# Regrouping the fp32 transposes in the q, k, v stage of a gated attention and token-mixer kernel

## The chip, the cores and the metric

One core of a Trainium2 chip runs the whole kernel. The metric is the device time of one execution in microseconds (us); less is better. TensorE is called PE in the rows, VectorE DVE, ScalarE ACT, GpSimd POOL and SyncE SP; SP issues the DMAs here.

## The reference

For x of 2048 tokens by 640 channels the result is `g * a + (1 - g) * b`, with one gate g per token:

```python
g = sigmoid((x * gate_w).sum(-1, keepdims=True))
q = (x @ wq).reshape(B, S, 32, 20).transpose(0, 2, 1, 3)
k, v = x @ wk, x @ wv                      # one key and one value head, 20 wide
p = softmax(einsum("bhqd,bkd->bhqk", q, k) * 20 ** -0.5)
a = einsum("bhqk,bkd->bhqd", p, v).transpose(0, 2, 1, 3).reshape(B, S, 640) @ wo
h = layernorm(x)                           # over the channels
u = gelu(einsum("bsd,sf->bdf", h, w1) + b1)   # mixes the tokens, F = 1728
b = (einsum("bdf,fs->bds", u, w2) + b2).transpose(0, 2, 1)
```

The change touches the first two lines of this alone: the transposes of x that the projections read, and the transposes of v and of the gate's sum.

## The kernel before

The kernel runs three stages one after the other: the q, k, v stage (about the first 95 us), a lead stage, and the long attention loop into which the token mixer's matmuls are woven. All engines follow the order in which the instructions were written (a manual schedule), so each engine takes its instructions in program order, and a wait in front holds back all that stands behind it on that engine.

The q, k, v stage works on four blocks of 512 tokens (`sb`, lines 430 to 475). For each block the tokens' 640 channels, in five chunks `c` of 128, have to lie across the partitions. `transpose_x` (L312) does that on TensorE: four fp32 transposes of 128x128 fill one PSUM bank of 128x512. `split_x` (L307) then reads the bank twice, ScalarE for the high part (L309) and VectorE for the low part (L310). All matmuls of the projections take such high and low parts. `project` (L324) is a row of matmuls of 512 columns that add up in one bank.

A block goes like this. First comes `pk`, ten matmuls that give k, v and the gate's sum. `split_kv` takes them out: ScalarE copies one half (L346), VectorE adds the other (L347), and the sum lies in `kv` (blocks 0 and 1) or `kept` (blocks 2 and 3). Then five projections of q follow, m = 0 to 4. The x of the next block is turned beside them, in groups of chunks that stand ahead of a projection. After each projection `split_q` takes the one before it out (L339 on ScalarE, L340 on VectorE) and stores it. `turn_v` (L361) turns `kv` by four transposes (L364) into one bank, which is read by a copy to `v_sb` (ScalarE L368 in block 0, VectorE L366 else) and by a copy to `z_col` (VectorE L369). The layer norm of the block runs between all this on VectorE, ScalarE and POOL: its `ht` tiles (L276) share two buffers, so the third scaling waits until POOL has taken the low parts of the first (L290).

Two PSUM pools of four banks each serve the stage: `psa` (tiles `pp`, the projections and chunk 4 of x) and `pst` (tiles `pt`, the other chunks of x, and v):

```python
pts = [(pst if c < 4 else psa).tile([P, NB], F32, name="pt" if c < 4 else "pp") for c in cs]
```

In block 0 the projections m = 0 to 2 are mostly done ahead, so that the row of m = 2 has only five matmuls left, and the group of m = 3 follows that of m = 2 closely.

Of the kernel before, what the change touches and what calls it, by code (L numbers as in the profile page):

```python
# [20 lines left out]
DC = D // P  # L21
# [4 lines left out]
NQB = S // NB  # L26
# [22 lines left out]
def mix_kernel(ctx: ExitStack, tc: tile.TileContext, A_x, A_wq, A_wk, A_wv, A_wo,  # L49
# [130 lines left out]
    def new_qmax(n):  # L180
        if n < NU and n not in qmax:
            qmax[n] = load_q(n, "qmx")
# [9 lines left out]
    with tc.tile_pool(name="pa", bufs=1) as pa, \  # L192
# [9 lines left out]
        def load_x(sb):  # L202
            for st in range(4 * sb, 4 * sb + 4):
                nc.sync.dma_start(out=xts[st], in_=x[st * P:(st + 1) * P, :])
# [102 lines left out]
        def split_x(sb, c, pt):  # L307
            th, tl = x_tiles(sb, c)
            nc.scalar.activation(th, pt, AF.Copy)  # L309
            nc.vector.tensor_sub(tl, pt, f32(th))  # L310

        def transpose_x(sb, cs):  # L312
            pts = [(pst if c < 4 else psa).tile([P, NB], F32, name="pt" if c < 4 else "pp") for c in cs]
            for i in range(4):
                for c, pt in zip(cs, pts):
                    nc.tensor.transpose(pt[:, i * P:(i + 1) * P], xts[4 * sb + i][:, c * P:(c + 1) * P], ident)
            return [(sb, c, pt) for c, pt in zip(cs, pts)]

        def project(steps, pp=None, more=False):
            first = pp is None  # L320
            if first:
                pp = psa.tile([P, NB], F32, name="pp")
            for n, (w, t) in enumerate(steps):
                nc.tensor.matmul(pp, w, t, start=first and n == 0, stop=not more and n == len(steps) - 1)  # L324
            return pp

        def q_parts(m, ts):
            cols = slice(m * P, (m + 1) * P)
            return [[(wq_hi[:, c, cols], ts[c][0]) for c in range(DC)],
                    [(wq_hi[:, c, cols], ts[c][1]) for c in range(DC)],  # L330
                    [(wq_lo[:, c, cols], ts[c][0]) for c in (0, 3, 1, 4, 2)]]

        def split_q(sb, m, pp):
            if (sb, m) == (NQB - 1, DC - 1):
                qh, ql = (xin[0][:, i, :NB].bitcast(F32R) for i in range(2))
            else:
                qh = paw.tile([P, NB], F32R, name="qh")
                ql = paw.tile([P, NB], F32R, name="ql")
            nc.scalar.activation(qh, pp, AF.Copy)  # L339
            nc.vector.tensor_sub(ql, pp, f32(qh))  # L340
            for j, t in enumerate((qh, ql)):
                nc.sync.dma_start(out=q_scr[j, m * P:(m + 1) * P, sb * NB:(sb + 1) * NB], in_=f32(t))

        def split_kv(sb, pp):
            kv = kvs[max(0, sb - 1)][:64, :]
            nc.scalar.activation(kv, pp[64:, :], AF.Copy)  # L346
            nc.vector.tensor_add(kv, kv, pp[:64, :])  # L347
            k_hi = pa.tile([DH, NB], F32R, name="k_hi")
            k_lo = pa.tile([DH, NB], F32R, name="k_lo")
            nc.scalar.activation(k_hi, kv[:DH, :], AF.Copy)  # L350
            nc.gpsimd.tensor_sub(k_lo, kv[:DH, :], f32(k_hi))
            return kv, k_hi, k_lo

        def store_k(sb, k_hi, k_lo):
            cols = slice(sb * NB, (sb + 1) * NB)
            for b in range(2):
                for j, t in enumerate((k_hi, k_hi, k_lo)):
                    o = 64 * b + DH * j
                    nc.sync.dma_start(out=f32(kst[o:o + DH, cols]), in_=f32(t))

        def turn_v(sb):  # L361
            pv = pst.tile([P, 4, P], F32, name="pt")
            for i in range(4):
                nc.tensor.transpose(pv[:, i, :], kvs[max(0, sb - 1)][:, i * P:(i + 1) * P], ident)  # L364
            if sb:
                nc.vector.tensor_copy(v_sb[:, 4 * sb:4 * sb + 4, :DH], pv[:, :, 32:32 + DH])  # L366
            else:
                nc.scalar.activation(v_sb[:, :4, :DH], pv[:, :, 32:32 + DH], AF.Copy)  # L368
            nc.vector.tensor_copy(z_col[:, 4 * sb:4 * sb + 4], pv[:, :, 32 + DH])  # L369

        def turn_bias():
            pb = pst.tile([P, NB], F32, name="pt")
            nc.tensor.transpose(pb[:, :P], bb, ident)
            nc.vector.tensor_copy(bias, pb[:, :32])
# [17 lines left out]
        def first_block():  # L392
            ahead = [psa.tile([P, NB], F32, name="pp") for _ in range(QW // P)]

            def turn(c):
                nc.gpsimd.tensor_copy(wq_hi[:, c, :QW], wqs[c])
                split_x(*transpose_x(0, (c,))[0])

            nc.gpsimd.tensor_copy(wq_hi[:, 0, :QW], wqs[0])
            th, tl = x_tiles(0, 0)  # L400
            for a in range(2):
                pt = pst.tile([P, NB], F32, name="pt")
                cols = slice(a * 2 * P, (a + 1) * 2 * P)
                for i in range(2):
                    nc.tensor.transpose(pt[:, i * P:(i + 1) * P], xts[2 * a + i][:, :P], ident)
                nc.scalar.activation(th[:, cols], pt[:, :2 * P], AF.Copy)
                nc.vector.tensor_sub(tl[:, cols], pt[:, :2 * P], f32(th[:, cols]))
            for c in range(DC):
                if c == 0:
                    for i in range(2):  # L410
                        nc.tensor.matmul(warm, kst[:, :P], kst[:, :NB], start=True, stop=True)
                    first_q(c, 0, ahead)
                if c + 1 < DC:
                    turn(c + 1)
                for j in range(c == 0, 2):
                    first_q(c, j, ahead)
                wq_low(c, slice(0, QW), wqs[c])
            load_x(1)
            split_wkv()
            for c in range(DC):  # L420
                nc.scalar.activation(wq_hi[:, c, QW:], wqs2[c], AF.Copy)
            for c in (0, 3, 1, 4, 2):
                wq_low(c, slice(QW, D), wqs2[c])
            norm = layer_norm(0)
            for _ in range(3):
                next(norm)
            return ahead, norm

        due = None
        for sb in range(NQB):  # L430
            ahead, norm = first_block() if sb == 0 else ([], layer_norm(sb))
            ts = [xT[sb, c] for c in range(DC)]
            if 0 < sb < NQB - 1:
                load_x(sb + 1)
            pk = project([(wkv_s[:, c, :], t) for c in range(DC) for t in ts[c]])
            if due:
                split_q(*due)
            kv, k_hi, k_lo = split_kv(sb, pk)
            store_k(sb, k_hi, k_lo)
            if sb:  # L440
                next(norm)
            for m in range(DC):
                turned = []
                if sb + 1 < NQB and m > 1 and (sb, m) != (2, DC - 1):
                    turned = transpose_x(sb + 1, ((0, 1), (2, 3), (4,))[m - 2])
                p = q_parts(m, ts)
                if m < len(ahead):
                    pp = project(p[2], ahead[m])
                elif m < DC - 1:
                    pp = project(p[0] + p[1] + p[2])  # L450
                else:
                    pp = project([p[r][c] for c in range(DC) for r in range(3)])
                if m == (not sb):
                    turn_v(sb)
                if m:
                    split_q(*due)
                due = sb, m, pp
                for t in turned:
                    split_x(*t)
                if sb == 1 and m == 1:  # L460
                    turn_bias()
                if sb == 1 and m == 0:
                    w1_load(3)
                if sb == 2 and 0 < m < 4:
                    w1_upto(m)
                if sb == 3 and m == 1:
                    w1_upto(4)
                    new_qmax(0)
                if sb == 3 and m == 3:
                    gates()  # L470
                for _ in range(2 if sb == 0 and m == 1 else 1 + (sb and m > 1 or sb == 3)):
                    next(norm, None)
            if sb == 2:
                for t in transpose_x(3, (4,)):
                    split_x(*t)
# [721 lines left out]
    m = len(ph)  # L1197
# [304 lines left out]
```

## Time and profile before

| | |
|---|---|
| median of 3 runs | 1594.0 us (1593.82 to 1594.34) |
| the profiled execution's own time | 1594.53 us |
| its span, first to last instruction | 1592.4 us |
| TensorE (PE) busy | 1587.0 us, 100% of the span |
| VectorE (DVE) busy | 1348.2 us, 85% |
| ScalarE (ACT) busy | 1293.0 us, 81% |
| POOL busy | 866.5 us, 54% |
| mean granted TensorE clock | 1.000 |

A matmul's end is modelled and lies past the start of the next one, so in the rows below a step of TensorE is read from start to start: a matmul of 512 columns takes 0.23 us of it (eight in a row from 30.19 us to 32.06 us), though its row shows 0.4 us. A row of the timeline merges neighbours of one kind; its first number is the start of the first of them.

### The profile page before, as it was taken

Reading aid. Unit: us, or ns where it says so; the run is one execution under the profiler, and the core shown is the slowest. Engines: PE = TensorE matmul, PEld = TensorE weight load, DVE = VectorE, ACT = ScalarE, POOL = GpSimd, SP = SyncE. Lnnn points to the kernel's source line nnn. Section 1 sums busy time; section 2 is a strip of 40 time slices with the busy share of each in tenths; the row PEclk is TensorE's granted clock in tenths of the full one; section 3 lists DMA queues with packets and bytes.
Section 4 is the critical chain, followed back from the end, with each engine's and each line's share of the span. In section 5 each row is a group of like instructions: output and inputs, shape, how many; then the busy total and the mean of one; then the engine's idle time right before and its main releaser. Section 6 shows DMA issues by size and latency. Waiting matters only on the chain.

```text
span 1592.4 us, 39402 instructions
## 1 busy us (share of the span) xinstructions
PE 1587.0 (100%) x14800; PEld 1120.8 (70%) x14800; DVE 1348.2 (85%) x2316; ACT 1293.0 (81%) x2585; POOL 866.5 (54%) x983
## 2 busy tenths in 40 slices
PE   9999999999999999999999999999999999999999
PEld 7889776677667766666666666666666666666676
DVE  6688999999999999888888888888888888766643
ACT  4458888888888888888888888888888888999975
POOL 6478777678777777544544434454544433344420
PEclk9999999999999999999999999999999999999999
DMA  7665223223333222222222121222222112235521
GB/s 220 194 181 142 67 75 85 80 69 89 88 85 88 79 74 65 66 73 82 74 75 67 50 70 54 79 74 82 74 74 64 58 51 64 86 121 181 178 83 62
DMA packets 179705, 144.25 MB, mean 91 GB/s; under 512 B 34127, under 2 KB 141260, under 8 KB 179516
## 3 DMA queue, kind: packets, MB, share of 16 engines
q1 hardware_dynamic: 179228, 141.42, 31.1%
q8 instruction: 116, 1.90, 0.5%
q14 instruction: 73, 0.60, 0.1%
q10 hardware_dynamic: 288, 0.33, 0.1%
HBM read 107.70 MB, written 32.15 MB: 88 GB/s over the span
## 4 chain that ended last, share of the span: by engine, by line
PE 99%; DVE 0%; issue 0%; DVEq 0%
PE s L884 14%; PE ms L884 12%; PE g L962 11%; PE ms L554 9%; PE s L554 8%; PE s L747 8%; PE g L1165 8%; PE ms L747 7%; PE pp L324 5%; PE o L884 4%; PE o L747 3%; PE o L554 3%; PE s L812 2%; PE g L1101 2%; PE s L1056 1%; PE ms L583 1%
## 5 line engine op out<-in xcount | busy, mean ns | idle before, releaser
L560 DVE TENSOR_REDUCE mp<-ms 128x1 f32<-128x512 f32 x910 | 596.9, 681 | 63.5 <-PE ms L554 32.8
L560 DVE TENSOR_REDUCE mp<-s 128x1 f32<-128x512 f32 x786 | 519.0, 681 | 72.3 <-PE s L554 41.0
L758 ACT ACTIVATE p<-s 128x512 f32<-128x512 f32 x914 | 536.5, 635 | 12.6 <-PE s L747 8.8
L758 ACT ACTIVATE p<-ms 128x512 f32<-128x512 f32 x794 | 474.2, 634 | 4.7 <-PE ms L747 3.3
L897 POOL TENSOR_TENSOR acc<-acc,part 128x512 f32<-128x512 f32 x213 | 275.3, 1292 | 307.6 <-ACT part L896 304.5
L747 PE MATMUL s<-qst,kst 62*128 62x512 f32 x918 | 351.8, 407 | 0.0
L554 PE MATMUL ms<-kst,qmx 60*128 60x512 f32 x910 | 349.6, 407 | 0.0
L747 PE MATMUL ms<-qst,kst 62*128 62x512 f32 x795 | 309.8, 409 | 0.0
L1165 PE MATMUL g<-slot,wh 64*128 64x320 f32 x1344 | 308.5, 309 | 0.0
L554 PE MATMUL s<-kst,qmx 60*128 60x512 f32 x786 | 304.6, 411 | 0.3 <-DVE mp L560 0.3
L884 PE MATMUL s<-p,v_sb 128*32 128x512 f32 x1856 | 223.2, 598 | 0.0
L1165 PEld LDWEIGHTS g<-slot,wh 64*128 64x128 f32 x1344 | 222.4, 184 | 0.0
L150 POOL TENSOR_TENSOR wl<-wr,wh 128x512 fp32r<-128x512 f32 (+1 forms) x168 | 207.7, 1237 | 12.8 <-ACT wh L147 0.9
L1165 PE MATMUL g<-slot,wl 64*128 64x320 f32 x672 | 212.5, 316 | 0.0
L554 PEld LDWEIGHTS ms<-kst,qmx 60*128 60x128 f32 x910 | 166.0, 185 | 58.5 <-ACT p L758 33.7
L884 PE MATMUL ms<-p,v_sb 128*32 128x512 f32 x1688 | 204.6, 598 | 0.0
L560 DVE TENSOR_REDUCE mp<-o 128x1 f32<-128x512 f32 x261 | 178.0, 682 | 30.4 <-PE o L554 20.4
L758 ACT ACTIVATE p<-o 128x512 f32<-128x512 f32 x307 | 195.0, 635 | 3.2 <-PE o L747 2.7
L962 PE MATMUL g<-u,wh 64*128 64x320 f32 x864 | 195.1, 308 | 0.0
L962 PE MATMUL g<-slot,wh 64*128 64x320 f32 x864 | 195.1, 308 | 0.0
L747 PEld LDWEIGHTS s<-qst,kst 62*128 62x128 f32 x918 | 169.0, 185 | 25.1 <-DVE mp L560 11.7
L554 PEld LDWEIGHTS s<-kst,qmx 60*128 60x128 f32 x786 | 143.2, 185 | 60.7 <-ACT p L758 34.4
(289 smaller groups left out, 3140.2 us busy)
## 6 DMA issues: line engine op xcount, KB each, us to landing
wr<-in_B_w_dram SPq DMA_DIRECT2D x136, 256.0 KB
qmx<-q_scr SPq DMA_DIRECT2D x192, 80.0 KB
qst<-q_scr SPq DMA_DIRECT2D x192, 80.0 KB
ot<-l_scr SPq DMA_DIRECT2D x120, 64.0 KB
y_scr<-yo SPq DMA_DIRECT2D x16, 320.0 KB
slot<-o_scr SPq DMA_DIRECT2D x16, 320.0 KB
o_scr<-ot SPq DMA_DIRECT2D x124, 40.0 KB
o_scr<-acc SPq DMA_DIRECT2D x124, 40.0 KB
```

Source lines behind the costliest of these rows:

```text
L150: nc.gpsimd.tensor_sub(wl[:, :nv], wr[:, :nv], f32(wh[:, :nv]))
L324: nc.tensor.matmul(pp, w, t, start=first and n == 0, stop=not more and n == len(steps) - 1)
L554: nc.tensor.matmul(ms, qmax[n][64 * b:64 * b + 60, pr, qt * P:(qt + 1) * P], kst[64 * b:64 * b + 60, kq * NB:(kq + 1) * NB], start=True, s ...
L560: r = nc.vector.tensor_reduce(mtiles[n][:, c, kq:kq + 1], ms, axis=AX.X, op=ALU.max)
L747: nc.tensor.matmul(s, kst[64 * b:64 * b + 62, kb * P:(kb + 1) * P], q[64 * b:64 * b + 62, pr, :], start=True, stop=True)
L758: e = nc.scalar.activation(p, s, AF.Exp, scale=SCALE)
L812: nc.tensor.matmul(pu[r][:, :HD2], w[rows, c, :], h[rows, st, :], start=(st == 0 and k == 0), stop=(st == NS - 1 and k == len(terms) - 1))
L884: nc.tensor.matmul(o[32 * hh:32 * hh + 32, :], v_sb[:, kb + i, :], ptiles.pop((u, hh)), start=opened and i == 0, stop=(i == len(us) - 1) a ...
L897: nc.gpsimd.tensor_add(sums[0], sums[0], part)
L962: other_tile(half, nc.tensor.matmul(hold["p"][:, :HD2], w[r, i, :], u[d][r, fc, :], start=(hold["n"] == 1), stop=(hold["n"] == 6 * FC - 3)))
L1101: other_tile(half, nc.tensor.matmul(hold["p"][:, :HD2], o[r, c, :], w[r, c, d * HD2:(d + 1) * HD2], start=(hold["n"] == 1), stop=(hold["n" ...
L1165: other_tile(half, nc.tensor.matmul(hold["p"][:, :HD2], w[r, st % HS, :], h[d][r, st, :], start=(hold["n"] == 1), stop=(hold["n"] == 6 * NS)))
```

## The change

In blocks 0 and 1 the five chunks of the next block's x are turned in two groups, chunks 0 and 1 ahead of projection m = 2 and chunks 2, 3 and 4 ahead of m = 3, where there were three groups, the last of them chunk 4 ahead of m = 4. Block 2 keeps its groups. `turn_v` stood behind projection m = 1 in block 0 and behind m = 0 in the other blocks. It now stands behind the first group of x, ahead of projection m = 2, in blocks 0 to 2, and ahead of projection m = 0 in block 3, right behind `pk`.

```diff
             for m in range(DC):
                 turned = []
-                if sb + 1 < NQB and m > 1 and (sb, m) != (2, DC - 1):
-                    turned = transpose_x(sb + 1, ((0, 1), (2, 3), (4,))[m - 2])
+                if sb + 1 < NQB and 1 < m < DC - 1:
+                    turned = transpose_x(sb + 1, ((0, 1), (2, 3) if sb == 2 else (2, 3, 4))[m - 2])
+                if m == (2 if sb < 3 else 0):
+                    turn_v(sb)
                 p = q_parts(m, ts)
...
                     pp = project([p[r][c] for c in range(DC) for r in range(3)])
-                if m == (not sb):
-                    turn_v(sb)
                 if m:
                     split_q(*due)
                 due = sb, m, pp
```

The first place is TensorE in block 0, the group ahead of projection m = 3. `pt` are banks of `pst`, `pp` is one of `psa`, `xb` holds the x of block 1; the name in brackets is the semaphore that the instruction waits for, DVE_49 being VectorE's.

```order
 L316 MATMUL pt<-ident,xb 128x128
 L316 MATMUL pt<-ident,xb 128x128 [waits DVE_49]
-L316 MATMUL pt<-ident,xb 128x128 x6
+L316 MATMUL pp<-ident,xb 128x128
+L316 MATMUL pt<-ident,xb 128x128 x2
+L316 MATMUL pp<-ident,xb 128x128
+L316 MATMUL pt<-ident,xb 128x128 x2
+L316 MATMUL pp<-ident,xb 128x128
+L316 MATMUL pt<-ident,xb 128x128 x2
+L316 MATMUL pp<-ident,xb 128x128
```

The group grows from 8 to 12 transposes, and its second transpose (the first of chunk 3) waits for VectorE in both programs. What it waits for is the reading of v's bank: five tiles of `pst` are taken from v, chunks 0 and 1, and chunks 2 and 3, and there are four banks. Of those four the only one that is read by then is v's, and its last reader is the copy to `z_col`.

The second place is VectorE in block 0, where that copy stands. The `ht` rows are the layer norm's scalings of block 0, `ql` the low parts of q; Pool_49 is POOL's semaphore and DMAHW1_49 that of a DMA queue.

```order
 L269 TENSOR_TENSOR rstd<-r_284,r_285 128x4 [waits DVE_49]
-L369 COPY z_col<-pt 128x4 [waits Activation_49]
 L340 TENSOR_TENSOR ql<-pp,qh 128x512 [waits Activation_49]
 L276 TENSOR_SCALAR ht<-xa,mv,rstd 128x640 [waits DVE_49]
 L276 TENSOR_SCALAR ht<-xa,mv,rstd 128x640 [waits DMAHW1_49]
 L276 TENSOR_SCALAR ht<-xa,mv,rstd 128x640 [waits DVE_49,Pool_49]
+L369 COPY z_col<-pt 128x4 [waits Activation_49]
 L340 TENSOR_TENSOR ql<-pp,qh 128x512 [waits Activation_49]
```

The copy to `z_col` stood ahead of one `ql` and three scalings and now stands behind them, the third of which waits for POOL.

The third place is TensorE at the start of block 3, where `pk` ends and projection m = 0 begins.

```order
 L324 MATMUL pp<-xT_hi,wkv_s 128x512 [waits Activation_49]
 L324 MATMUL pp<-xT_lo,wkv_s 128x512 [waits DVE_49]
+L364 MATMUL pt<-ident,kept_75 128x128 [waits DVE_49]
+L364 MATMUL pt<-ident,kept_75 128x128 x3
 L324 MATMUL pp<-qst,wq_hi 128x512 x2
 L324 MATMUL pp<-qmx,wq_hi 128x512
```

The transposes of v, which read what `split_kv` makes of the bank that the row above them fills, stood 15 matmuls further down and now stand directly behind that row. The order of SP's DMAs is the same in both programs, and so is the order of every engine behind the q, k, v stage.

## Rows read from the trace of the kernel before

**Rows 1.** The page's first part: busy us (share of the span) xinstructions of each engine.

```profile
PE 1587.0 (100%) x14800; PEld 1120.8 (70%) x14800; DVE 1348.2 (85%) x2316; ACT 1293.0 (81%) x2585; POOL 866.5 (54%) x983
```

**Rows 2.** The waits of PE over the whole span: us in total, times, longest.

```profile
PE pp L208 <- DVE kst L78: 1.5, 1, 1.5
PE s L554 <- DVE mp L560: 0.3, 1, 0.3
```

**Rows 3.** Timeline of PE in block 0: start us, us, engine, line, out<-in, count.

```profile
19.46 0.60 PE L364 MATMUL pt<-ident,kv 128*128 128x128 f32 x4
19.89 1.04 PE L316 MATMUL pt<-ident,xb 128*128 128x128 f32 x8
20.68 0.95 PE L324 MATMUL pp<-slot,wq_lo 128*128 128x512 f32 x3
...
21.93 1.04 PE L316 MATMUL pt<-ident,xb 128*128 128x128 f32 x8
22.73 1.17 PE L324 MATMUL pp<-slot,wq_hi 128*128 128x512 f32 x4
...
26.30 0.60 PE L316 MATMUL pp<-ident,xb 128*128 128x128 f32 x4
26.65 0.72 PE L324 MATMUL pp<-slot,wq_hi 128*128 128x512 f32 x2
```

**Rows 4.** Timeline of DVE in block 0; in brackets idle time before, and its releaser.

```profile
19.53 1.16 DVE L269 TENSOR_TENSOR rstd<-r,r 128x4 f32<-128x4 f32 x1
20.62 0.15 DVE L369 COPY z_col<-pt 128x4 f32<-128x4 f32 x1
20.85 0.69 DVE L340 TENSOR_TENSOR ql<-pp,qh 128x512 fp32r<-128x512 f32 x1
21.46 1.13 DVE L276 TENSOR_SCALAR ht<-xa,mv,rstd 128x640 f32<-128x640 f32 x2
24.39 1.15 DVE L276 TENSOR_SCALAR ht<-xa,mv,rstd 128x640 f32<-128x640 f32 x1 [1.81 <-POOL slot L290]
...
26.07 1.27 DVE L310 TENSOR_TENSOR slot<-pt,slot 128x512 fp32r<-128x512 f32 x2
```

**Rows 5.** Timeline of ACT in block 0.

```profile
18.70 0.63 ACT L350 ACTIVATE k_hi<-kv 20x512 fp32r<-20x512 f32 x1 [0.74 <-DVE kv L347]
20.09 0.24 ACT L368 ACTIVATE v_sb<-pt 128x80 f32<-128x80 f32 x1 [0.76 <-PE pt L364]
20.23 0.59 ACT L339 ACTIVATE qh<-pp 128x512 fp32r<-128x512 f32 x1
22.10 1.56 ACT L289 ACTIVATE slot<-ht 128x320 fp32r<-128x320 f32 x4 [1.28 <-DVE ht L276]
```

**Rows 6.** Timeline of POOL in block 0.

```profile
22.65 5.31 POOL L290 TENSOR_TENSOR slot<-ht,slot 128x320 fp32r<-128x320 f32 x6 [1.98 <-ACT slot L289]
```

**Rows 7.** Timeline of PE at the start of block 3.

```profile
77.12 0.40 PE L324 MATMUL pp<-xT_lo,wkv_s 128*128 128x512 f32 x1
77.35 0.63 PE L324 MATMUL pp<-qst,wq_hi 128*128 128x512 f32 x2
...
80.83 0.60 PE L364 MATMUL pt<-ident,kept 128*128 128x128 f32 x4
```

**Rows 8.** Timeline of ACT at the start of block 3.

```profile
77.55 0.59 ACT L346 ACTIVATE kept<-pp 64x512 f32<-64x512 f32 x1 [1.25 <-PE pp L324]
```

**Rows 9.** Timeline of DVE at the start of block 3.

```profile
78.18 0.68 DVE L347 TENSOR_TENSOR kept<-kept,pp 64x512 f32<-64x512 f32 x1 [1.05 <-ACT kept L346]
```

**Rows 10.** Timeline of PE at the start of the span.

```profile
1.45 2.50 PE L208 MATMUL pp<-kst 128*128 128x512 f32 x5 [1.45 <-DVE kst L78]
...
5.56 1.44 PE L390 MATMUL pp<-slot,wq_hi 128*128 128x512 f32 x3
...
7.19 0.94 PE L390 MATMUL pp<-slot,wq_hi 128*128 128x512 f32 x3
```

**Rows 11.** Lead stage: window us, busy us (x) of PE, PEld, DVE, ACT, POOL; clock, DMA.

```profile
95.00:200.00 105.00, 104.65 (x1164) 88.01 (x1162) 97.64 (x151) 82.22 (x166) 83.13 (x92) 1.00 0.51 129
```

## The prediction

> **What bounds the kernel now.** I read the busy times first: TensorE is busy for 1587.0 of 1592.4 us, and no other engine comes above 85% [rows 1]. The list of TensorE's waits came next, to see whether that busy time hides pauses: over the whole span it holds two, 1.5 us at the start for a memset and 0.3 us [rows 2]. So TensorE sets the time, and whatever makes it wait or gives it more to do is paid nearly in full, since there are no waits further on in which a delay could sink. Then I read the timeline of each engine around the moved instructions. In the q, k, v stage TensorE steps from one group to the next without a pause [rows 3], because each of its operands is ready well ahead. The question for each moved instruction is thus how late its operand or its bank becomes ready now.
>
> **The change part by part.** The number of transposes, matmuls, copies and DMAs stays the same. Three things can cost.
>
> *First, the bank of chunk 3 in block 0.* The second transpose ahead of projection m = 3 writes the first part of chunk 3, into the bank that v left. Before, v stood ahead of the first group of x, and its last reader, the copy to `z_col`, ran from 20.62 us for 0.15 us [rows 4]. TensorE wanted the bank at 21.93 us, the start of the group, plus one step of 0.11 us (eight transposes take 22.73 - 21.93 = 0.80 us [rows 3], most of it in steps of 0.11 us), so at 22.04 us, and did not wait. Now the copy stands behind one `ql` and three scalings. Its new time is worked out along the rows of VectorE, ScalarE and POOL. With the copy gone from its front, `ql` starts when `rstd` lets it, at 20.62 instead of 20.85 us, 0.23 us earlier; its `qh` is ready by then, for on ScalarE it no longer stands behind the wait for v and can follow `k_hi`, which ends at 18.70 + 0.63 = 19.33 us [rows 5]. The two scalings that started at 21.46 us [rows 4], the four copies of ScalarE from 22.10 us [rows 5] and POOL's subtractions from 22.65 us [rows 6] follow on each other and move by the same 0.23 us. The third scaling waited 1.81 us for two of those subtractions and ran from 24.39 us for 1.15 us, to 25.54 us [rows 4]; now to 25.31 us. The copy behind it ends near 25.4 us, VectorE's small instructions overlapping by some 0.08 us (`rstd` ends at 20.69, the copy starts at 20.62 [rows 4]). ScalarE's copy to `v_sb`, which must precede it, follows the four copies and is done near 23.6 us. An engine starts some 0.04 us after its releaser (78.14 to 78.18 us [rows 8, 9]), so TensorE goes on at 25.44 us: a stall of 25.44 - 22.04 = 3.4 us, where there was none. Behind the waiting transpose stand all of TensorE's instructions, so nothing else fills it. The other ways to free a bank are later still: chunks 0 and 1 are read by VectorE from 26.07 us [rows 4].
>
> The bounds: if the third scaling takes what each of the first two took, 1.13 / 2 = 0.57 us, the stall is 0.58 us shorter, 2.8 us; if the 0.23 us are not gained and starting costs 0.1 us, it is 3.7 us. I take 3.4 us, the row of that very scaling.
>
> The Trainium skill (SBUF — State Buffer, section Who interferes with whom) says that VectorE in its two-port mode and POOL exclude each other, and that whoever starts first keeps the shared ports for its whole instruction. The doubled row of 1.15 us beside POOL's subtractions agrees. By that rule the scaling meets a subtraction again and the sum below stands; if it came first, 0.57 us would hold and the sum would be 5.0 us.
>
> *Second, v in block 3.* The transposes of v stand right behind `pk` now. `pk`'s last matmul starts at 77.12 us and the next instruction can start at 77.35 us [rows 7]. ScalarE takes one half out from 77.55 us for 0.59 us [rows 8], VectorE adds the other from 78.18 us and ends at 78.18 + 0.68 = 78.86 us [rows 9]. Before, TensorE asked for the sum at 80.83 us [rows 7], 2 us after it was there, with 15 matmuls as cover; now the cover is gone. The transposes can start at 78.90 us, and with nothing in front under which their first weights load I add 0.1 us, then 4 x 0.11 us, so that projection m = 0 starts at 79.45 instead of 77.35 us: 2.1 us later. The 0.35 us that four transposes took further down (26.65 - 26.30 [rows 3] for such a group) are saved there, which leaves 1.75 us. Bounds: 1.55 us, the bare wait with the group costing what it did, and 2.0 us with another 0.25 us for the restart. I take 1.75 us.
>
> *Third, joined groups.* Eight transposes take 0.80 us and four take 0.35 us, 1.15 us apart from each other [rows 3]. The first of a group costs little, since its weights load under a long matmul, and each further one 0.11 us, so that four more in the same group cost 0.80 - 0.35 = 0.45 us. That is 0.10 us for each join. There are four: chunk 4 in blocks 0 and 1, v in blocks 1 and 2. In block 0, v and x already stood in one run of twelve (19.46 to 20.68 us [rows 3]), only in the other order. Together 0.4 us; the bounds are 0 and 0.4 us.
>
> At nothing I cost v's transposes in blocks 1 and 2, apart from the join: they move about two projections behind the addition that they read, and chunk 3's bank there has a whole projection of 15 matmuls, 3.5 us, between v and the group that wants it, while only short copies stand ahead of `z_col`. The earlier chunk 4 gains nothing, since `pk` of the next block did not wait for it. The DMAs keep their order and move with TensorE.
>
> The sum: 3.4 + 1.75 + 0.4 = 5.55 us. The profiled execution took 1594.53 us, 0.53 us over the median of the three runs; with the change it would be 1600.1 us, and the median 1599.5 us. From the lower and upper bounds (4.35 and 6.1 us) this case alone reaches from 1598.3 to 1600.3 us.
>
> **The rivals.** *The clock falls in the first stall.* At the start of the span matmuls of 512 columns take some 0.42 us each (three from 5.56 to 6.83 us), from 7.19 us on about 0.23 us [rows 10]: first the lower level of 1.2 GHz, then 2.4 GHz. The lower one lasted for 5.4 us of work from 1.45 us on, after idleness. If a stall of 3.4 us brings it back for as long, half of that is lost, 2.7 us: 1602.2 us, and 1604.9 us if it happens in block 3 too. For it speaks that no wait in the trace is as long; against it that the granted clock was 1.000 over the span and the stall is short beside the work around it. Chance 0.15. The Trainium skill (TensorE: Matmul & The Clock Gate, section Why this matters for your kernels) warns of this very thing, idle gaps between bursts of matmuls that bring the slow level back; no row here has a gap by which to test it.
>
> *The first stall does not come.* If `z_col`'s copy is done in time after all, or chunk 3 gets another bank, 1.75 + 0.4 = 2.15 us remain: 1596.2 us. Against it stand VectorE's fixed order and the 1.81 us wait for POOL in front [rows 4]. Chance 0.11.
>
> *The delay is made good in the lead stage, so that the time is not longer.* While TensorE stands, VectorE, ScalarE and POOL finish the layer norms and the weights' splits that do not need it. From 95 to 200 us VectorE is busy for 97.64 of 105 us [rows 11]; if TensorE is paced there by waits that its modelled ends hide, it could run faster with the others ahead. This decides from 5.3 us gained in 105 us, 5% of the stage. Then the time is 1594.3 us or less. Against it: TensorE is busy for 104.65 us there [rows 11], only 0.3 us of waiting are listed [rows 2], and most of VectorE's work there reads what TensorE has just made. Chance 0.06.
>
> **How the numbers follow.** My forecast has 0.68, the clock 0.15, the missing stall 0.11, the head start 0.06. The predicted time is that of the forecast, 1599.5 us. The range goes from 1596.0 us, which takes in the missing stall, to 1602.8 us, which takes in one fall of the clock. A measurement of this kernel tells about 0.2%, 3.2 us, from no change, so slower begins at 1597.2 us. The forecast and the clock make 0.83 of it, and a partial stall 0.01 more: 0.84. The missing stall and most of the head start fall within 0.2%: 0.13. Faster keeps 0.03.
>
> **What would show it.** In the profile after, TensorE's waits should hold one of about 3.4 us at line 316 for VectorE's `z_col` (line 369), near 22 us, and one of about 1.6 us at line 364 for line 347, near 81 us. `z_col` in block 0 should start near 25.3 us, behind three scalings. Twelve transposes in one group of blocks 0 and 1 should take some 1.25 us where nothing holds them. From 95 us on the stages should be as long as before, only later by 5 to 6 us. The prediction is wrong if the first wait is under 2.5 us, if matmuls of 512 columns behind it take 0.42 us, or if the lead stage gets shorter.

## The result and the profile after

The changed kernel took 1601.03 us (median of 6 runs, 1599.06 to 1602.06), the kernel before 1593.99 us on the same occasions. The ratio is 1.0041 with a 95% interval of [1.0028, 1.0054]: slower, by more than 0.2%. The runs of the changed kernel fall in two groups, two at 1599.06 and 1599.13 us and four from 1600.8 to 1602.06 us. The profiled execution is of the second group (1600.8 us, span 1598.9 us). One run of one experiment below, 1712.28 us with v of blocks 0 and 3 put back, was in a slower state from start to end (mean granted clock 0.851) and stands in no ratio.

TensorE's waits over the whole span, after (us in total, times, longest; the answer to [rows 2]):

```profile
PE pt L316 <- DVE z_col L369: 3.6, 1, 3.6
PE pp L208 <- DVE kst L78: 1.5, 1, 1.5
PE pt L364 <- DVE kept L347: 1.4, 1, 1.4
PE s L554 <- DVE mp L560: 0.3, 1, 0.3
PE pt L316 <- DMA xa<-in_A_x_dram: 0.2, 1, 0.2
```

The two waits of [rows 2] are still there, and two long new ones stand beside them, at the two places that were named, with a short one for a DMA that was not. TensorE's timeline in block 0, after (start us, us; the answer to [rows 3]):

```profile
19.27 1.03 PE L316 MATMUL pt<-ident,xb 128*128 128x128 f32 x8
20.14 0.60 PE L364 MATMUL pt<-ident,kv 128*128 128x128 f32 x4
...
21.74 0.27 PE L316 MATMUL pt<-ident,xb 128*128 128x128 f32 x1
25.59 0.36 PE L316 MATMUL pt<-ident,xb 128*128 128x128 f32 x1 [3.58 <-DVE z_col L369]
25.76 0.40 PE L316 MATMUL pp<-ident,xb 128*128 128x128 f32 x1
25.95 0.64 PE L316 MATMUL pt<-ident,xb 128*128 128x128 f32 x2
...
27.66 0.42 PE L316 MATMUL pp<-ident,xb 128*128 128x128 f32 x1
27.73 1.84 PE L324 MATMUL pp<-slot,wq_hi 128*128 128x512 f32 x4
29.41 0.40 PE L324 MATMUL pp<-xT_hi,wq_hi 128*128 128x512 f32 x1
29.64 1.08 PE L324 MATMUL pp<-slot,wq_hi 128*128 128x512 f32 x4
```

Chunk 3's first transpose stands still for 3.58 us, and behind it the group crawls: a transpose takes 0.21 us from start to start instead of 0.11 us, and four matmuls from 27.73 us take 1.68 us up to the next row, 0.42 us each. From 29.41 us on a matmul is back at 0.23 us. The reader is to see two losses in one place, the wait and the slowness after it. The second is the clock, as three stretches of the same profile show (window us, busy us of PE, PEld, DVE, ACT and POOL with counts, granted clock, DMA):

```profile
21.80:25.60 3.80, 0.22 (x3) 0.01 (x1) 2.03 (x5) 3.23 (x9) 2.98 (x4) 1.00 0.34 93
25.80:29.10 3.30, 3.30 (x14) 3.07 (x13) 3.30 (x6) 2.54 (x6) 2.04 (x3) 0.50 1.09 302
29.20:34.00 4.80, 4.80 (x22) 3.92 (x21) 2.08 (x4) 1.38 (x4) 1.72 (x2) 1.00 0.29 93
```

While TensorE did almost nothing the granted clock was still 1.00 in this profile; just after it went on it was 0.50, the lower level of 1.2 GHz, and then 1.00, the upper level of 2.4 GHz, again. VectorE's timeline in block 0, after (the answer to [rows 4]):

```profile
20.84 0.68 DVE L340 TENSOR_TENSOR ql<-pp,qh 128x512 fp32r<-128x512 f32 x1
21.43 1.13 DVE L276 TENSOR_SCALAR ht<-xa,mv,rstd 128x640 f32<-128x640 f32 x2
24.33 1.13 DVE L276 TENSOR_SCALAR ht<-xa,mv,rstd 128x640 f32<-128x640 f32 x1 [1.77 <-POOL slot L290]
25.39 0.15 DVE L369 COPY z_col<-pt 128x4 f32<-128x4 f32 x1
```

The third scaling waits for POOL as before, `z_col` now starts as it ends, at 25.39 us, and TensorE goes on at 25.59 us, 0.05 us after the end of `z_col`. Block 3, TensorE and then VectorE, after (the answer to [rows 7, 9]):

```profile
82.26 0.40 PE L324 MATMUL pp<-xT_lo,wkv_s 128*128 128x512 f32 x1
84.05 0.66 PE L364 MATMUL pt<-ident,kept 128*128 128x128 f32 x4 [1.40 <-DVE kept L347]
84.46 0.71 PE L324 MATMUL pp<-qst,wq_hi 128*128 128x512 f32 x2
```

```profile
83.32 0.68 DVE L347 TENSOR_TENSOR kept<-kept,pp 64x512 f32<-64x512 f32 x1 [1.05 <-ACT kept L346]
```

The listed wait is 1.40 us since the modelled end of the last matmul covers a part of the pause; from start to start, 82.26 to 84.05 us, it is 1.79 us where a step takes 0.23 us.

Where the span's 6.4 us are, by the start of each block's `pk` on TensorE and that of the lead stage (14.82, 30.19, 52.66, 74.92 and 95.26 us before; 14.63, 35.40, 57.83, 80.07 and 102.03 us after):

| stretch | before, us | after, us | difference |
|---|---|---|---|
| start to `pk` of block 0 | 14.82 | 14.63 | -0.19 |
| block 0 | 15.37 | 20.77 | +5.40 |
| block 1 | 22.47 | 22.43 | -0.04 |
| block 2 | 22.27 | 22.24 | -0.03 |
| block 3, to the lead stage | 20.34 | 21.97 | +1.63 |
| lead stage to the end | 1497.18 | 1496.84 | -0.35 |

Of block 0's 5.40 us the pause is 25.59 - 21.74 - 0.11 = 3.74 us, from start to start less one step; the other 1.7 us are the lower clock behind it.

### The profile page after: what moved, and what is told of

The parts are those of the page before. It is cut to its first block, busy times and chain, and to the rows that moved or that the text cites. A ratio compares the mean times of both kernels' runs of the same rounds, so it can differ in the third digit from the quotient of the medians.

```text
span 1598.9 us, 39402 instructions
## 1 busy us (share of the span) xinstructions
PE 1588.3 (99%) x14800; PEld 1121.2 (70%) x14800; DVE 1347.4 (84%) x2316; ACT 1293.3 (81%) x2585; POOL 866.3 (54%) x983
## 4 chain that ended last, share of the span: by engine, by line
PE 98%; DVE 1%; DMA 0%; issue 0%; POOL 0%; SPq 0%; ACT 0%; DVEq 0%
PE s L884 14%; PE ms L884 12%; PE g L962 11%; PE ms L554 9%; PE s L554 8%; PE s L747 8%; PE g L1165 8%; PE ms L747 7%; PE pp L324 4%; PE o L884 4%; PE o L554 3%; PE o L747 3%; PE s L812 2%; PE g L1101 2%; PE s L1056 1%; PE ms L583 1%
## 5 line engine op out<-in xcount | busy, mean ns | idle before, releaser
L554 PE MATMUL ms<-kst,qmx 60*128 60x512 f32 x910 | 349.5, 407 | 0.0
L554 PE MATMUL s<-kst,qmx 60*128 60x512 f32 x786 | 304.3, 410 | 0.3 <-DVE mp L560 0.3
L554 PEld LDWEIGHTS ms<-kst,qmx 60*128 60x128 f32 x910 | 165.9, 185 | 58.5 <-ACT p L758 33.5
L554 PEld LDWEIGHTS s<-kst,qmx 60*128 60x128 f32 x786 | 143.1, 185 | 60.7 <-ACT p L758 34.4
```

What stands on the lines that cost most here:

```text
L554: nc.tensor.matmul(ms, qmax[n][64 * b:64 * b + 60, pr, qt * P:(qt + 1) * P], kst[64 * b:64 * b + 60, kq * NB:(kq + 1) * NB], start=True, s ...
```

## The experiments

The theory before the runs was: the change costs two stalls of TensorE, the first behind `z_col` and the second behind the addition of k and v in block 3; they add up; and the first one brings the clock down in most runs. Each experiment below starts from the changed kernel.

**v of block 0 put back.**

```diff
-                if m == (2 if sb < 3 else 0):
+                if m == (2 if sb < 3 else 0) and sb:
                     turn_v(sb)
...
                     pp = project([p[r][c] for c in range(DC) for r in range(3)])
+                if m == 1 and sb == 0:
+                    turn_v(sb)
```

> In block 0 alone the transposes of v go back behind projection m = 1, so that the copy to z_col stands ahead of the scalings again; the rest is the changed kernel. Theory (the 3.58 us wait for z_col is the first stall, and standing still is what brings the clock down): no wait at line 316 for z_col, the granted clock is 1.000 in every run, and what is left is the wait in block 3: 1594.0 + 1.6 = 1595.6 us. Rival (the long runs of transposes bring the clock down, 12 in a row in two places of block 0): the clock still falls in about half of the runs and those lie 1.7 us higher, at 1597.3 us. Second rival (chunk 3 waits for another reader of its bank): a wait of over 2 us stays at line 316 and the time stays over 1598 us.

It took 1595.62 us (11 runs, 1594.92 to 1596.73) against 1594.12 us, ratio 1.001 [1.0001, 1.0019]. Its waits of TensorE (lines behind the edit are two higher, L556 is L554):

```profile
PE pp L208 <- DVE kst L78: 1.5, 1, 1.5
PE pt L364 <- DVE kept L347: 1.4, 1, 1.4
PE s L556 <- DVE mp L562: 0.3, 1, 0.3
```

The wait for `z_col` is gone and the clock stays up, though block 0 still has a run of twelve transposes in two places; the mean granted clock is 1.000 in all 11 runs. So v's place in block 0 makes the first stall and the runs of transposes do not lower the clock. What is left, 1.5 us, is block 3.

**v of block 3 put back.**

```diff
-                if m == (2 if sb < 3 else 0):
+                if m == 2 and sb < 3:
                     turn_v(sb)
...
                     pp = project([p[r][c] for c in range(DC) for r in range(3)])
+                if m == 0 and sb == 3:
+                    turn_v(sb)
```

> In block 3 alone the transposes of v go back behind projection m = 0; the rest is the changed kernel. Theory (the two stalls add up on TensorE): the wait at line 364 for line 347 goes, and each run is 1.6 us shorter than the changed kernel's of the same clock: about 1597.5 us with the clock at 1.000 and 1599.2 us with one fall, in a mixture. Rival (the delay of block 0 is there anyway and block 3's wait lies hidden behind it, or is given back in the lead stage): the same time as the changed kernel, 1599.1 to 1602 us.

Median 1599.13 us, ratio 1.0032 [1.002, 1.0045]: one run at 1597.59 us and four from 1599.01 to 1600.64 us. Each group lies 1.5 to 2 us below that of the changed kernel, so the second stall is paid on its own, and nothing further on gives it back. The run at 1597.59 us, 3.5 us above the kernel before, is the first stall alone, though one run only. The profile is of a run with the fall (1599.01 us), and the fall comes at another moment than in the changed kernel's. TensorE, then a window (columns as above):

```profile
25.59 0.48 PE L316 MATMUL pt<-ident,xb 128*128 128x128 f32 x1 [3.34 <-DVE z_col L369]
```

```profile
25.00:25.50 0.50, 0.00 (x0) 0.00 (x0) 0.50 (x3) 0.21 (x1) 0.50 (x2) 0.50 0.63 201
```

The granted clock is 0.50 here from 25.0 us on, while TensorE still stands; it goes on at 25.59 us. So the clock can fall within the pause as well as just behind it.

**Both put back, the joined groups left.**

```diff
-                if m == (2 if sb < 3 else 0):
+                if m == 2 and 0 < sb < 3:
                     turn_v(sb)
...
                     pp = project([p[r][c] for c in range(DC) for r in range(3)])
+                if (sb, m) in ((0, 1), (3, 0)):
+                    turn_v(sb)
```

> v goes back in blocks 0 and 3, so that only the joined groups of blocks 0, 1 and 2 are left of the change. The prediction's term for the joins: 4 x 0.10 = 0.4 us over the kernel before, 1594.4 us. Rival (each end of a group costs some 0.09 us in the matmul behind it, which a join saves, so that the joins come out even): 1594.0 us within 0.1 us. In both the clock stays at 1.000.

1594.2 us (median of 11 runs; the ten in the ratio lie from 1593.4 to 1595.21 us) against 1594.12 us, ratio 1.0001 [0.9992, 1.001]. The interval does not exclude 0.4 us, 0.025%. The profiles do: blocks 1 and 2, which hold three of the four joins, take 22.42 and 22.23 us here (`pk` at 30.19, 52.61 and 74.84 us) and 22.43 and 22.24 us in the changed kernel, against 22.47 and 22.27 us before. In all eight profiles with the joins they take 22.41 to 22.44 us and 22.23 to 22.24 us. The reason is seen on TensorE in block 1 of the changed kernel:

```profile
44.79 1.03 PE L316 MATMUL pt<-ident,xa 128*128 128x128 f32 x8
45.67 0.60 PE L364 MATMUL pt<-ident,kv 128*128 128x128 f32 x4
46.02 1.17 PE L324 MATMUL pp<-slot,wq_hi 128*128 128x512 f32 x4
47.02 0.39 PE L324 MATMUL pp<-xT_hi,wq_hi 128*128 128x512 f32 x1
47.25 1.10 PE L324 MATMUL pp<-slot,wq_hi 128*128 128x512 f32 x4
48.19 0.40 PE L324 MATMUL pp<-xT_lo,wq_hi 128*128 128x512 f32 x1
```

The four matmuls behind the group take 47.02 - 46.02 = 1.00 us, the next four 48.19 - 47.25 = 0.94 us. Most of what the end of a group saves on the transposes is paid in the matmul behind it, so that a join comes out about even: the group of twelve takes 46.02 - 44.79 = 1.23 us where groups of eight and four take 1.15 us, and one end of a group with its 0.06 us is saved.

**The third scaling behind `z_col`.** One step of block 0's layer norm goes from behind projection m = 1 to behind m = 2; TensorE's order is that of the changed kernel.

```diff
-                for _ in range(2 if sb == 0 and m == 1 else 1 + (sb and m > 1 or sb == 3)):
+                for _ in range(2 if sb == 0 and m == 2 else 1 + (sb and m > 1 or sb == 3)):
```

> The changed kernel with one step of block 0's layer norm moved from behind projection m = 1 to behind m = 2, so that the third scaling (which waits for POOL) stands behind the copy to z_col; TensorE's order is that of the changed kernel. Theory (the wait for POOL in front of z_col is what makes the stall long): z_col starts near 23.1 us, behind ScalarE's copy to v_sb, the wait at line 316 is 1.3 us instead of 3.58 us, the clock stays at 1.000, and the time is 1599.1 - 2.3 = 1596.8 us. Rival (the runs of transposes bring the clock down): the wait shrinks as well but the clock falls in about half of the runs, to 1598.5 us.

1596.75 us (11 runs, 1596.55 to 1597.58), ratio 1.0018 [1.0009, 1.0027], without a fall of the clock. VectorE and then TensorE in block 0:

```profile
23.20 0.16 DVE L369 COPY z_col<-pt 128x4 f32<-128x4 f32 x1 [0.50 <-ACT v_sb L368]
```

```profile
22.34 0.27 PE L316 MATMUL pt<-ident,xb 128*128 128x128 f32 x1
23.42 0.33 PE L316 MATMUL pt<-ident,xb 128*128 128x128 f32 x1 [0.81 <-DVE z_col L369]
```

One small copy, put ahead of one scaling that waits for POOL, takes 4.3 us off the changed kernel's median, the fall of the clock included. TensorE's order is untouched, so the length of the stall is set by what stands in front of `z_col` on VectorE, and now by ScalarE's copy to `v_sb`, for which `z_col` waits 0.50 us. (The step takes two of ScalarE's copies with it, from in front of `v_sb`, which starts at 22.95 us instead of 23.53 us.) The time was met, in part by luck: the wait is 0.81 us instead of the 1.3 us expected, and a wait of 0.28 us for the DMA of `xb`, which was not expected, stands beside it.

**All four scalings ahead of `z_col`.** The same line the other way.

```diff
-                for _ in range(2 if sb == 0 and m == 1 else 1 + (sb and m > 1 or sb == 3)):
+                for _ in range(3 if sb == 0 and m == 1 else 1 + (sb and m > 1 or sb == 3)):
```

> The changed kernel with one more step of block 0's layer norm behind projection m = 1, so that all four scalings stand ahead of the copy to z_col. Theory (the stall follows z_col, and a longer standing still brings the clock down more surely): z_col starts near 27.3 us, the wait at line 316 is 5.5 us, without a fall the time would be 1599.1 + 1.9 = 1601.0 us, and as the clock falls in every run the time is about 1602.7 us. Rival (whether the clock falls does not hang on the length of the stall): the same share of runs as in the changed kernel keeps the clock at 1.000, with 1601.0 us.

1603.19 us, five runs from 1602.68 to 1603.53 us, ratio 1.0056 [1.0044, 1.0069]. The wait is 5.05 us, where 5.5 us were expected, and `z_col` starts at 27.22 us. Three rows of its TensorE:

```profile
22.10 0.27 PE L316 MATMUL pt<-ident,xb 128*128 128x128 f32 x1
27.42 0.41 PE L316 MATMUL pt<-ident,xb 128*128 128x128 f32 x1 [5.05 <-DVE z_col L369]
27.62 0.42 PE L316 MATMUL pp<-ident,xb 128*128 128x128 f32 x1
```

No run lies near the 1601.0 us that would go with a clock that stays up; the clock was lower behind the stall in the profile (0.50 from 27.6 to 30.9 us). Five runs alone do not show that a longer stall is surer to bring it down than the changed kernel's.

**The changed kernel again, beside that one.**

> The changed kernel itself, beside the one with the longer stall on the same chip. Theory (a stall of 3.58 us lies near the length at which the clock falls, so that it falls in some runs and not in others): two groups of runs again, near 1599.1 us with the clock at 1.000 and 1.7 us or more above it with a fall. Rival (the two groups come from the chip or the hour): one group alone.

1601.2 us, ratio 1.0046 [1.0032, 1.006], five runs from 1600.65 to 1602.79 us: one group, the slower one. With the first six, 9 of 11 runs lie there. That is what the rival expected of this batch and not what the theory did; whether a chip or the hour has a part in the share stays open.

**The stall filled with work.** Fourteen matmuls whose sums nobody reads, ahead of the group of projection m = 3 in block 0.

```diff
                 turned = []
+                if (sb, m) == (0, 3):
+                    fill = psa.tile([P, NB], F32, name="pp")
+                    for i in range(14):
+                        nc.tensor.matmul(fill, wq_hi[:, 0, :P], ts[0][0], start=True, stop=True)
                 if sb + 1 < NQB and 1 < m < DC - 1:
```

> The changed kernel with 14 more matmuls of 512 columns on TensorE ahead of the group of projection m = 3 in block 0; their sums are never read. They take 14 x 0.23 = 3.2 us, where TensorE stood still for 3.1 to 3.6 us. Theory (it is TensorE's standing still that brings the clock down, and the stall itself is paid once): the wait at line 316 for z_col shrinks to some 0.3 us, the time lost there stays 3.5 us, the granted clock is 1.000 in every run and the median is that of the changed kernel's runs without a fall, 1599.1 us, 2 us less than the changed kernel though it does more. Rival (the clock falls for the group of twelve transposes or for the wait as such): it falls in most runs as before, at about 1601 us. Second rival (the matmuls are an addition): 1604 us.

1599.17 us, six runs from 1598.68 to 1599.47 us, ratio 1.003 [1.0018, 1.0043]. TensorE in block 0 (L447 is the fill):

```profile
22.19 3.38 PE L447 MATMUL pp<-slot,wq_hi 128*128 128x512 f32 x14
25.41 0.50 PE L316 MATMUL pt<-ident,xb 128*128 128x128 f32 x2
25.75 0.27 PE L316 MATMUL pp<-ident,xb 128*128 128x128 f32 x1
...
26.73 0.27 PE L316 MATMUL pp<-ident,xb 128*128 128x128 f32 x1
26.76 1.18 PE L324 MATMUL pp<-slot,wq_hi 128*128 128x512 f32 x4
```

The fill ends as `z_col` comes, the group of twelve takes 26.76 - 25.41 = 1.35 us instead of 27.73 - 25.59 = 2.14 us for eleven, and in the stretch where the changed kernel had 0.50 the granted clock is 1.00:

```profile
25.80:29.10 3.30, 3.30 (x21) 2.90 (x20) 3.30 (x6) 3.13 (x8) 2.16 (x4) 1.00 1.07 281
```

All runs are at the level of the changed kernel's faster group. The useless work costs nothing where TensorE would stand still, and the median is 2.0 us below the changed kernel's 1601.2 us of the experiment above. `z_col` comes as late as it did and the transposes are the same, so it is TensorE's standing still that lowers the clock. One thing stays open: these six runs are from another chip than the other experiments, and no run of the changed kernel is known to be from that one. On one and the same chip, v of block 3 put back had the fall in four of five runs, and the two kernels without a long pause in block 0, v of block 0 put back and the third scaling behind `z_col`, had it in none of 22.

## Why the prediction was right, and where it was off

The time lies in the stated range, and the two stalls were named rightly. But the median is not the forecast's own case, in which the clock stays up: two of the first six runs were that, and four were the rival to which it gave 0.15. One of its own signs of being wrong came true in the profile, matmuls of 512 columns at 0.42 us behind the stall.

- **What bounds the kernel.** Right. TensorE's delays came out in full: from the lead stage to the end the two profiles differ by 0.35 us of 1497 us. The rival that the lead stage makes the delay good falls.
- **The first stall.** Right in place, cause and size: 3.4 us forecast from start to start, 3.74 us so counted in the profile (3.58 us as a listed wait), of which 0.19 us come from TensorE reaching block 0 that much earlier; 3.5 us as the one run that had it alone. `z_col` was forecast to start near 25.3 us and started at 25.39 us. Moving one scaling behind it and another ahead of it changed the wait to 0.81 and 5.05 us. The gain of 0.23 us on VectorE, a part of the working, was lost again: `rstd` now ended at 20.91 us instead of 20.69 us, and `ql` started at 20.84 us, as before.
- **The second stall.** Right in place and cause: 1.63 us in the profile, 1.5 us in the runs with block 0 put back, against 1.75 us. The 0.1 us that was added for the first weights does not show: TensorE went on 0.05 us after the addition's end, and the four transposes took 0.41 us.
- **The joined groups.** Wrong in size: 0.4 us forecast, none measured in blocks 1 and 2. The step that failed is that four more transposes in a group cost 0.45 instead of 0.35 us and that this is the whole difference; the matmuls behind each group, 0.06 us longer for the first four, were not counted.
- **The clock.** The mechanism was among the rivals, and its chance of 0.15 was far too low: 9 of 11 runs of the changed kernel have it. The argument against it, a stall short beside the work around it, does not hold. Its price, 2.7 us for one fall, was too high, since the start of the span was taken for a measure: there the lower level lasted for 5.4 us, here 0.50 was granted from about 25.8 to 29.2 us, and half of that is the 1.7 us left over in block 0. Between the medians it is 2.0 us. The changed kernel's slowest runs, 1602.06 and 1602.79 us, also have its lowest mean clock, 0.998 and 0.997 where its other falls have 0.999; whether the lower level lasted longer in them or came twice is not shown, for none was profiled.
- **The sum.** 1599.5 us forecast against 1601.03 us. The runs without the fall, 1599.1 us, are the forecast less the joins; the median is this with the fall on top. The upper end of the forecast's own case was added up wrongly: 1594.0 + 6.1 is 1600.1 us, not 1600.3 us.
- **Not foreseen:** x of the next block is asked for 0.43 us sooner in block 0, since v no longer stands ahead of it. In three of the profiles, the filled kernel's among them, this shows as a wait of 0.3 us for the DMA of `xb`; in the profile of the changed kernel that is shown above there is none there.

That chunk 3 could be given a bank of its own was not tried, nor any version in which v stands behind the first group with its wait covered; with the joins at nothing no run points to a version below the kernel before.

## What to carry to other kernels

A tile that frees a PSUM bank is only as early as its last reader in that reader's own queue: before moving a producer, look at what stands ahead of the copy that empties its bank, and add up the waits of that queue. A move that brings a consumer right up to its producer can cost the whole chain between them, however short its instructions are. And a pause of the engine that bounds a kernel can cost twice, once as time and once as clock.

## What the runs showed of the hardware

In the profile of the changed kernel the granted clock was 1.00 from 21.8 to 25.6 us, with 0.22 us of work, and 0.50 from 25.8 to 29.1 us with TensorE busy throughout; with v of block 3 put back it was 0.50 already within the pause, from 25.0 us. The kernels whose profiles list pauses of 0.8 to 1.4 us had no fall in 22 runs, those of 3.1 to 3.6 us had one in 13 of 16, and that of 5.05 us in five of five, a run without a profile being counted by its time. At the lower level the fp32 transposes also take twice as long, 0.21 against 0.11 us. The figure of the granted clock does not tell all: over 1.45 to 6.83 us of the kernel before it reads 1.00, though the matmuls from 5.56 us take 0.42 us, so the steps are to be read beside it. And 14 matmuls more made the kernel 2.0 us faster.
